# A gated scan and two MLPs in one kernel on one Trainium2 core: subtractions moved to GpSimd, the first pair's rows in 4 KB pieces, f rows and sigmoids earlier, and other ways out for two last blocks

## The chip, the core and the metric

The kernel runs on one core of a Trainium2 chip. TensorE multiplies matrices, VectorE and ScalarE work element by element and read the matmul results from PSUM, GpSimd works element by element from SBUF, and SyncE only issues transfers. Transfers are also issued by ScalarE and GpSimd; each issuer has a queue of its own, and each engine runs its instructions in the order of the program. The metric is the device time of one execution in microseconds (us).

## The reference, cut to what matters

```python
f = lower_bound + (1.0 - lower_bound) * sigmoid(f_logit)   # x, f_logit: 6080 tokens x 256
i = 1.0 - f
for t in range(6080):                                      # the gated scan
    h = f[t] * h + i[t] * x[t]
    y[t] = h
h = y @ w_in                                               # 256 x 2048
y = (h * sigmoid(1.702 * h)) @ w_out                       # layer 1, 2048 x 256
h = y @ w_in_2
g = h if h >= 1 else (0 if h <= -1 else (h + 1) ** 2 / 4)
out = g @ w_out_2                                          # layer 2
```

The weights come as 64-bit floats, 2 words of 32 bits each; x, f_logit and the result are 32-bit.

## The kernel before

**Tiling.** The 6080 tokens are six pairs of two blocks; a block has 480 tokens in the first pair and 512 in the others. Features lie on the 128 partitions, two halves of 128, and tokens along the rows. Every matrix operand is kept as a high half rounded for TensorE (`h`) and a low half, the difference to the exact value (`l`); a product is three matmuls, `wh*mh`, `wl*mh` and `wh*ml` (`three`, L406). ScalarE makes the high half as a cast (L191 for weights, L517 for activations), VectorE the low half as a subtraction (L195 for weights, L521 for activations).

**Order.** The order of all engines is written out by hand. The work of one pair is eight groups of 256 of the 2048 inner columns. The first pair uses `plain_group`: for each of four pieces (P11, P21, P12, P22: block b, half u of the inner columns) two products into a bank, then the down products of the group before, and then whatever `run(s, k)` holds for group s, place k. Later pairs, and all of layer 2, use `group`, which needs seven products for the same result in place of eight. `also(s, k, ...)` and `in_place(4 * s + k, ...)` put work into these places.

**The start.** Before group 0 stands a written order: weight units are loaded and taken from their 64-bit form (`take_apart`, `scale_exponent`, `put_together`, `weight_value`, then `weight_high` and `weight_low`); unit ("i", 0, 0) first, ("i", 0, 1) and ("o", 0, 0) half way. There are 16 units in layer 1, j = 0 to 7 of "i" and "o"; the 15 behind the first are spread over the groups of the first pair, where seven staging tiles take the loads. The blocks of the first pair are loaded by rows (`load_rows`, SP, pieces of 512 bytes), turned by TensorE's transposes (`turn_half`, L286), and scanned: `start_gate` (sigmoid, ScalarE, from PSUM), `forget`, `start_input` (VectorE), `scan` (VectorE), `scan_high`, `scan_low`. The blocks of later pairs are loaded by `load_tokens` in 128-byte pieces, four transfers each, in a blocked order that VectorE's 32 x 32 transposes undo; `sigmoid_tokens` does the sigmoid in place on ScalarE. The sigmoid and the Gelu need different tables of ScalarE, so `sigmoid_tokens` inside the groups has a table load before it, and the next Gelu has another one. The tiles of `load_rows` and `load_tokens` share two buffers each for x and f.

**The ends.** `keep_block` takes the result of a block out of PSUM when its last down product is done. In layer 1 it is copied to two `ev` tiles (halves e = 0 on ScalarE, L469, e = 1 on VectorE, L471) and written to a scratch in DRAM, from which `fetch` reads it for layer 2; the tag `ev` has two buffers. In layer 2 it is turned by VectorE's 32 x 32 transposes (L479) and written in 128-byte pieces, four transfers a block; the last pair's by SP and ScalarE in turn. The last block of all goes half by half through `store_half` (L489, L491), in eight transfers by SP and ScalarE.

Of the kernel before, what the change touches and what calls it, by code (L numbers as in the profile page):

```python
# [14 lines left out]
P = 128  # L15
Q = 32
# [28 lines left out]
def tile_gated_scan_two_mlps(  # L45
# [147 lines left out]
    def weight_low(u):  # L193
        high, low = unit_parts(u)
        nc.vector.tensor_tensor(low, joined.pop(u), high.bitcast(F32), ALU.subtract)  # L195
# [73 lines left out]
    def load_rows(what, b, g):  # L269

        t0, n = blocks[b]
        m = n // 4
        if g == 0:
            raw[what, b] = pool.tile([P, ND, 4, P], F32, tag=f"r{what}", bufs=2, name=f"rows_{what}{b}")
        nc.sync.dma_start(
            out=raw[what, b][:m, g],
            in_={"x": x, "f": f_logit}[what][t0 : t0 + n, g * P : (g + 1) * P].rearrange(
                "(c p) d -> p c d", p=m
            ),
        )  # L280

    def turn_half(b, g, places):
        m = blocks[b][1] // 4
        for what, p in zip("fx", places):
            for c in range(4):
                nc.tensor.transpose(  # L286
                    p[:, c * m : (c + 1) * m], raw[what, b][:m, g, c], ident[:m, :m]
                )
            turned[what, b, g] = p[:, : 4 * m]
# [3 lines left out]

    def start_gate(b, g):
        t = small("e0", "gate", b, g)
        nc.scalar.activation(t, turned.pop(("f", b, g)), AF.Sigmoid, scale=-1.0)
# [9 lines left out]
    def start_input(b, g):  # L306
        if g == 0:
            states[b] = [small("g", "state", b, h, 4) for h in range(ND)]
        nc.vector.scalar_tensor_tensor(
            states[b][g],  # L310
            gates.pop((b, g)),
# [149 lines left out]
    def keep_block(q, b):  # L461
        n = pairs[q % NPAIR][1]
        if q < NPAIR:
            between[q, b] = dram.tile([P, ND, n], F32, name=f"between{q}_{b}")
            for e in range(ND):
                t = pool.tile([P, n], F32, tag="ev", bufs=2, name=f"ev{q}_{b}_{e}")
# [6 lines left out]
        elif q == 2 * NPAIR - 1 and b:  # L473
            for e in range(ND):
                store_half(q, b, e)
        else:
# [3 lines left out]
            for k in range(P // Q):  # L480
                (nc.sync if q < 2 * NPAIR - 1 else (nc.sync, nc.scalar)[k % 2]).dma_start(
# [4 lines left out]
    def store_half(q, b, e):  # L486
        n = pairs[q % NPAIR][1]
        o = pool.tile([P, n], F32, tag=f"e{e}", bufs=2, name=f"o{q}_{b}_{e}")
        nc.vector.transpose(out=o, in_=ys.pop((q, b, e))[:, :n])  # L489
        for k in range(P // Q):  # L490
            (nc.sync, nc.scalar)[k % 2].dma_start(  # L491
                out=blocked(out, 2 * (q - NPAIR) + b, k)[:, e],
                in_=o[k * Q : (k + 1) * Q].rearrange("i (j c) -> i j c", c=Q),
            )
# [24 lines left out]
    def low(s, piece):  # L519
        h, l = parts[s, piece]  # L520
        nc.vector.tensor_tensor(l, G.pop((s, piece)), h.bitcast(F32), ALU.subtract)  # L521
# [149 lines left out]
    for n, (k, u) in enumerate(first_units):  # L671
        begun = {("i", 1): 4, ("o", 0): 3}.get((u[0], u[2]), 0)
# [192 lines left out]
```

## Time and profile before

| | |
|---|---|
| Time, median of 3 runs (lowest to highest) | 1035.28 us (1034.01 to 1037.02) |
| The profiled execution's own time | 1033.54 us |
| Its span, first to last instruction | 1031.7 us |
| TensorE busy | 998.3 us, 97% of the span |
| ScalarE, VectorE, GpSimd busy | 81%, 76%, 4% |
| Mean granted TensorE clock | 0.991 of full |
| Bytes moved | 71.77 MB, of which read from HBM 46.99 MB |

A busy TensorE counts matmuls that overlap, so 97% busy is not 97% of the peak; where it waits and where its clock falls is seen only by stretches. The rows below are of this one profiled execution; its own time is its span and 1.84 us around it.

### The profile page before, as it was taken

What the parts mean: (1) busy time and instruction counts of PE and PEld (TensorE: products, weight loads), DVE (VectorE), ACT (ScalarE), POOL (GpSimd) and SP (SyncE); (2) the same over time, 40 slices, a digit from 0 to 9 for tenths busy, and PEclk for the clock granted to TensorE, in tenths of its full rate; (3) what the DMA queues carried; (4) which work ended last, traced back from release to release, by engine and by line L of the source; (5) the groups of instructions that cost most, each with busy time, mean ns of one, the idle gap of its engine ahead of it and who ended that gap; (6) DMA issues with size and microseconds to landing.
All of it is one profiled execution on the core that took longest, in us unless ns stands there. A gap on an engine that the chain in (4) does not pass through costs nothing.

```text
span 1031.7 us, 12311 instructions
## 1 busy us (share of the span) xinstructions
PE 998.3 (97%) x4378; PEld 823.3 (80%) x4378; DVE 780.0 (76%) x1299; ACT 839.0 (81%) x1439; POOL 45.6 (4%) x80
## 2 busy tenths in 40 slices
PE   6799999999999999999999999999999999999995
PEld 4677888888888888888878888888888888888884
DVE  7889879778868878866667677768768767776664
ACT  5756787887887797877779889989988989998884
POOL 1100000000000000012210000000000000000000
PEclk9899999999999999999999999999999999999998
DMA  9932141054163351244561012002002002002002
GB/s 262 181 62 42 49 69 23 11 129 102 57 155 79 82 123 77 77 160 187 188 210 39 1 46 35 21 21 41 21 21 41 21 22 41 1 1 42 1 1 41
DMA packets 152278, 71.77 MB, mean 70 GB/s; under 512 B 134681, under 2 KB 139033, under 8 KB 152217
## 3 DMA queue, kind: packets, MB, share of 16 engines
q1 hardware_dynamic: 139528, 34.29, 16.6%
q0 software_dynamic: 8496, 36.18, 10.4%
q10 hardware_dynamic: 4192, 0.52, 0.3%
q8 instruction: 34, 0.56, 0.2%
q14 instruction: 28, 0.22, 0.1%
HBM read 46.99 MB, written 23.99 MB: 69 GB/s over the span
## 4 chain that ended last, share of the span: by engine, by line
PE 85%; DVE 6%; ACT 4%; DMA 2%; issue 1%; SPq 1%; DVEq 0%; ACTq 0%; POOLq 0%
PE y L406 45%; PE bank_b L406 17%; PE bank_a L406 11%; PE bank_c L406 11%; ACT gh L517 1%; ACT c L536 1%; ACT c L535 1%; DMA raw_x<-in_x 1%; DVE gl L521 1%; SPq L327 1%; DMA between<-ev 1%; DVE c L543 1%; DMA lb<-in_lower_bound 0%; DVE state L353 0%; DVE fieldsi L168 0%
## 5 line engine op out<-in xcount | busy, mean ns | idle before, releaser
L573 DVE TENSOR_TENSOR h<-bank_c,u 128x512 f32<-128x512 f32 (+1 forms) x176 | 120.4, 684 | 92.9 <-PE bank_c L406 63.9
L521 DVE TENSOR_TENSOR gl<-c,gh 128x512 fp32r<-128x512 f32 (+1 forms) x192 | 130.6, 680 | 10.9 <-ACT gh L517 8.7
L517 ACT CAST gh<-c 128x512 fp32r<-128x512 f32 (+1 forms) x192 | 117.6, 612 | 10.1 <-DVE c L543 9.7
L536 ACT ACTIVATE c<-c 128x512 f32<-128x512 f32 (+1 forms) x192 | 120.6, 628 | 6.1
L521 DVE TENSOR_TENSOR gl<-g,gh 128x512 fp32r<-128x512 f32 (+1 forms) x112 | 75.5, 675 | 42.8 <-ACT gh L517 42.4
L543 DVE SCALAR_TENSOR_TENSOR c<-c,h 128x512 f32<-128x512 f32 (+1 forms) x96 | 65.6, 684 | 55.9 <-ACT c L536 55.9
L531 ACT ACTIVATE h<-h 128x512 f32<-128x512 f32 x80 | 50.5, 631 | 56.7 <-DVE h L573 56.3
L517 ACT CAST gh<-g 128x512 fp32r<-128x512 f32 (+1 forms) x112 | 68.7, 613 | 15.8 <-PE y L406 12.6
L535 ACT ACTIVATE c<-h,half 128x512 f32<-128x512 f32 (+1 forms) x96 | 68.6, 715 | 9.0 <-DVE h L573 9.0
L593 ACT COPY bank_b<-bank_a 128x512 f32<-128x512 f32 (+1 forms) x88 | 50.3, 571 | 24.6 <-PE bank_a L406 23.9
L644 ACT COPY u<-bank_b 128x512 f32<-128x512 f32 (+1 forms) x88 | 50.9, 579 | 17.8 <-PE bank_b L406 17.5
L521 DVE TENSOR_TENSOR gl<-h,gh 128x512 fp32r<-128x512 f32 x80 | 54.8, 684 | 4.7 <-ACT gh L517 4.3
L517 ACT CAST gh<-h 128x512 fp32r<-128x512 f32 x80 | 49.7, 622 | 2.5
L623 ACT COPY u<-bank_b 128x512 f32<-128x512 f32 (+1 forms) x88 | 50.9, 578 | 0.1
L543 DVE SCALAR_TENSOR_TENSOR c<-c,bank_a 128x512 f32<-128x512 f32 (+1 forms) x48 | 32.7, 682 | 18.4 <-ACT c L536 18.4
L406 PE MATMUL y<-gh,wo_1l 128*128 128x512 f32 (+1 forms) x96 | 38.0, 396 | 1.4 <-DVE wo_1l L195 1.4
L406 PE MATMUL y<-gh,wo_0h 128*128 128x512 f32 (+1 forms) x96 | 37.5, 391 | 1.6 <-ACT gh L517 1.6
L406 PE MATMUL y<-gl,wo_5h 128*128 128x512 f32 (+1 forms) x96 | 37.3, 388 | 1.2 <-DVE gl L521 1.2
L406 PE MATMUL y<-gl,wo_2h 128*128 128x512 f32 (+1 forms) x96 | 37.4, 390 | 1.0 <-DVE gl L521 1.0
L406 PE MATMUL y<-gl,wo_3h 128*128 128x512 f32 (+1 forms) x96 | 37.3, 388 | 0.7 <-DVE gl L521 0.7
L406 PE MATMUL y<-gl,wo_0h 128*128 128x512 f32 (+1 forms) x96 | 37.3, 388 | 0.6 <-DVE gl L521 0.6
L406 PE MATMUL y<-gl,wo_1h 128*128 128x512 f32 (+1 forms) x96 | 37.9, 395 | 0.0
(377 smaller groups left out, 2953.8 us busy)
## 6 DMA issues: line engine op xcount, KB each, us to landing
kepti<-ahead_pi POOLq DMA_DIRECT2D x8, 896.0 KB, 3.9
stageo<-in_moe_w_out POOLq DMA_DIRECT2D x13, 512.0 KB, 4.2
stagei<-in_moe_w_in POOLq DMA_DIRECT2D x12, 512.0 KB, 4.2
raw_f<-in_f_logit SPq DMA_DIRECT2D x40, 128.0 KB, 4.2
raw_x<-in_x SPq DMA_DIRECT2D x40, 128.0 KB, 4.0
between<-ev SPq DMA_DIRECT2D x20, 256.0 KB, 2.7
y<-between SPq DMA_DIRECT2D x10, 512.0 KB, 3.4
out_y<-o SPq DMA_DIRECT2D x34, 128.0 KB, 3.5
```

The source lines that it names most:

```text
L327: nc.sync.dma_start(out=t[q * Q : (q + 1) * Q].rearrange("i g (j c) -> i g j c", c=Q), in_=blocked({"x": x, "f": f_logit}[what], b, q),)
L406: nc.tensor.matmul(o, lhsT=w, rhs=m, start=first and i == 0, stop=last and i == 2, skip_group_check=free,)
L517: nc.scalar.copy(parts[s, piece][0], G[s, piece])
L521: nc.vector.tensor_tensor(l, G.pop((s, piece)), h.bitcast(F32), ALU.subtract)
L531: nc.scalar.activation(G[s, piece], h, AF.Gelu_apprx_sigmoid)
L535: nc.scalar.activation(c, h, AF.Relu, scale=0.5, bias=half)
L536: nc.scalar.activation(c, c, AF.Square)
L543: nc.vector.scalar_tensor_tensor(c, c, 1.0, h, ALU.min, ALU.max)
L573: nc.vector.tensor_tensor(h, bank_c[:, : tokens(s)], u, ALU.add)
L593: nc.scalar.copy(b, a)
L623: nc.scalar.copy(u2, b)
L644: nc.scalar.copy(u3, b)
```

## The change

- `weight_low` and, in the first pair, `low` for the piece P21 run on GpSimd and no longer on VectorE (16 and 8 subtractions).
- `load_rows` loads a whole block in one transfer with 4 KB a partition, four tokens after one another. `turn_half` transposes from it, and `in_rows` views put the tokens back in order where ScalarE and VectorE read the transposes out of PSUM.
- f of blocks 2 and 3 is loaded by SP behind the first two weight units and ahead of the next four. `sigmoid_tokens` for them stands in the written order before group 0, ahead of the Gelu table. The steps of unit ("i", 0, 1) all stand before group 0, the last scan stands ahead of them, and the scans of the second pair come one to two places earlier.
- The last block of layer 1 is copied to the tiles `stagei` and `stageo`, which the weight units used before, instead of `ev`.
- In layer 2, two of the four transfers of the last pair's first block go by GpSimd instead of ScalarE. The last block is copied out by ScalarE and VectorE, turned to tokens by eight TensorE transposes, copied out again and written in 1 KB pieces by one transfer of ScalarE and one of SP (`store_last`).

```diff
@@ -192,7 +192,7 @@
 
     def weight_low(u):
         high, low = unit_parts(u)
-        nc.vector.tensor_tensor(low, joined.pop(u), high.bitcast(F32), ALU.subtract)
+        nc.gpsimd.tensor_tensor(low, joined.pop(u), high.bitcast(F32), ALU.subtract)
 
 
     def weight_sums(v):
@@ -266,17 +266,13 @@
     forgets = {}
     states = {}
 
-    def load_rows(what, b, g):
+    def load_rows(what, b):
 
         t0, n = blocks[b]
-        m = n // 4
-        if g == 0:
-            raw[what, b] = pool.tile([P, ND, 4, P], F32, tag=f"r{what}", bufs=2, name=f"rows_{what}{b}")
+        raw[what, b] = t = pool.tile([P, 4, D], F32, tag=f"r{what}", bufs=2, name=f"rows_{what}{b}")
         nc.sync.dma_start(
-            out=raw[what, b][:m, g],
-            in_={"x": x, "f": f_logit}[what][t0 : t0 + n, g * P : (g + 1) * P].rearrange(
-                "(c p) d -> p c d", p=m
-            ),
+            out=t[: n // 4],
+            in_={"x": x, "f": f_logit}[what][t0 : t0 + n, :].rearrange("(p c) d -> p c d", c=4),
         )
 
     def turn_half(b, g, places):
@@ -284,16 +280,19 @@
         for what, p in zip("fx", places):
             for c in range(4):
                 nc.tensor.transpose(
-                    p[:, c * m : (c + 1) * m], raw[what, b][:m, g, c], ident[:m, :m]
+                    p[:, c * m : (c + 1) * m], raw[what, b][:m, c, g * P : (g + 1) * P], ident[:m, :m]
                 )
-            turned[what, b, g] = p[:, : 4 * m]
+            turned[what, b, g] = p[:, : 4 * m].rearrange("q (c p) -> q p c", c=4)
 
     def small(tag, what, b, g, bufs=2):
         return pool.tile([P, blocks[b][1]], F32, tag=tag, bufs=bufs, name=f"{what}{b}_{g}")
 
+    def in_rows(t):
+        return t.rearrange("q (p c) -> q p c", c=4)
+
     def start_gate(b, g):
         t = small("e0", "gate", b, g)
-        nc.scalar.activation(t, turned.pop(("f", b, g)), AF.Sigmoid, scale=-1.0)
+        nc.scalar.activation(in_rows(t), turned.pop(("f", b, g)), AF.Sigmoid, scale=-1.0)
         gates[b, g] = t
 
     def forget(b, g):
@@ -307,8 +306,8 @@
         if g == 0:
             states[b] = [small("g", "state", b, h, 4) for h in range(ND)]
         nc.vector.scalar_tensor_tensor(
-            states[b][g],
-            gates.pop((b, g)),
+            in_rows(states[b][g]),
+            in_rows(gates.pop((b, g))),
             one_minus_lb[:, g : g + 1],
             turned.pop(("x", b, g)),
             ALU.mult,
@@ -463,7 +462,10 @@
         if q < NPAIR:
             between[q, b] = dram.tile([P, ND, n], F32, name=f"between{q}_{b}")
             for e in range(ND):
-                t = pool.tile([P, n], F32, tag="ev", bufs=2, name=f"ev{q}_{b}_{e}")
+                if q == NPAIR - 1 and b:
+                    t = pool.tile([P, n], F32, tag=("stagei", "stageo")[e], name=f"ev{q}_{b}_{e}")
+                else:
+                    t = pool.tile([P, n], F32, tag="ev", bufs=2, name=f"ev{q}_{b}_{e}")
                 y = ys.pop((q, b, e))[:, :n]
                 if e == 0:
                     nc.scalar.copy(t, y)
@@ -471,27 +473,45 @@
                     nc.vector.tensor_copy(t, y)
                 nc.sync.dma_start(out=between[q, b][:, e], in_=t)
         elif q == 2 * NPAIR - 1 and b:
-            for e in range(ND):
-                store_half(q, b, e)
+            store_last(q, b)
         else:
             o = pool.tile([P, ND, n], F32, tag="rf", bufs=2, name=f"o{q}_{b}")
             for e in range(ND):
                 nc.vector.transpose(out=o[:, e], in_=ys.pop((q, b, e))[:, :n])
             for k in range(P // Q):
-                (nc.sync if q < 2 * NPAIR - 1 else (nc.sync, nc.scalar)[k % 2]).dma_start(
+                (nc.sync if q < 2 * NPAIR - 1 else (nc.sync, nc.gpsimd)[k % 2]).dma_start(
                     out=blocked(out, 2 * (q - NPAIR) + b, k),
                     in_=o[k * Q : (k + 1) * Q].rearrange("i g (j c) -> i g j c", c=Q),
                 )
 
-    def store_half(q, b, e):
-        n = pairs[q % NPAIR][1]
-        o = pool.tile([P, n], F32, tag=f"e{e}", bufs=2, name=f"o{q}_{b}_{e}")
-        nc.vector.transpose(out=o, in_=ys.pop((q, b, e))[:, :n])
-        for k in range(P // Q):
-            (nc.sync, nc.scalar)[k % 2].dma_start(
-                out=blocked(out, 2 * (q - NPAIR) + b, k)[:, e],
-                in_=o[k * Q : (k + 1) * Q].rearrange("i (j c) -> i j c", c=Q),
-            )
+    def store_last(q, b):
+
+        t0, n = blocks[2 * (q - NPAIR) + b]
+        m = n // 4
+        rows = out[t0 : t0 + n, :].rearrange("(c p) d -> p c d", p=m)
+        turn = [bank_a, bank_b[LAST % 2 ^ 1]]
+        for e in range(ND):
+            t = pool.tile([P, n], F32, tag=f"e{e}", bufs=2, name=f"last{e}")
+            y = ys.pop((q, b, e))[:, :n]
+            if e == 0:
+                nc.scalar.copy(t, y)
+            else:
+                nc.scalar.copy(t[:, : n // 2], y[:, : n // 2])
+                nc.vector.tensor_copy(t[:, n // 2 :], y[:, n // 2 :])
+            for c in range(4):
+                nc.tensor.transpose(
+                    turn[c // 2][:m, (c % 2) * D + e * P : (c % 2) * D + (e + 1) * P],
+                    t[:, c * m : (c + 1) * m],
+                    ident,
+                )
+        for k, queue in enumerate((nc.scalar, nc.sync)):
+            o = pool.tile([P, 2, D], F32, tag="g", bufs=4, name=f"o_last{k}")
+            y = turn[k].rearrange("p (c d) -> p c d", c=2)
+            if k == 0:
+                nc.scalar.copy(o[:m], y[:m])
+            else:
+                nc.vector.tensor_copy(o[:m], y[:m])
+            queue.dma_start(out=rows[:, 2 * k : 2 * k + 2], in_=o[:m])
 
     def keep(b):
         for key in [key for key in to_keep if key[1] == b]:
@@ -518,7 +538,7 @@
 
     def low(s, piece):
         h, l = parts[s, piece]
-        nc.vector.tensor_tensor(l, G.pop((s, piece)), h.bitcast(F32), ALU.subtract)
+        (nc.gpsimd if s < NG and piece == P21 else nc.vector).tensor_tensor(l, G.pop((s, piece)), h.bitcast(F32), ALU.subtract)
 
     def begin(s, piece, bank=None):
 
@@ -669,7 +689,7 @@
 
     stages = ("stageo", "f0", "f1", "f2", "f3", "f4", "stagei")
     for n, (k, u) in enumerate(first_units):
-        begun = {("i", 1): 4, ("o", 0): 3}.get((u[0], u[2]), 0)
+        begun = {("i", 1): 6, ("o", 0): 3}.get((u[0], u[2]), 0)
         for i, step in enumerate(
             (take_apart, scale_exponent, put_together, weight_value, weight_high, weight_low)
         ):
@@ -701,13 +721,14 @@
                     also(s - 2, 0, load_tokens, "f", b)
                 also(s + (q > 1), 2, load_tokens, "x", b)
             for k in range(2):
-                also(s + (q > 1), 2 + (q == 1), sigmoid_tokens, 2 * q + k)
+                if q > 1:
+                    also(s + 1, 2, sigmoid_tokens, 2 * q + k)
             for k, (b, g) in enumerate((b, g) for b in (2 * q, 2 * q + 1) for g in range(ND)):
-                at = 4 * s + (5 + 5 * k if q == 1 else 8 + 4 * k)
+                at = 4 * s + (4 + 5 * k if q == 1 else 8 + 4 * k)
                 in_place(at, turn_gate, b, g)
                 in_place(at + 1, forget, b, g)
                 in_place(at + 2, turn_input, b, g)
-                in_place(at + 4 - (q > 1), scan, b, g)
+                in_place(at + 3, scan, b, g)
         else:
             for b in range(2):
                 also(s + 1 if q <= NPAIR + 1 else s - 1, 0, fetch, q, b)
@@ -759,11 +780,13 @@
     nc.gpsimd.dma_start(out=lb, in_=lower_bound.rearrange("(c p) -> p c", p=P))
     load_unit(("i", 0, 0), None, nc.sync)
     for b in range(2):
-        for g in range(ND):
-            load_rows("f", b, g)
-            load_rows("x", b, g)
-    for (_, u), tag in zip(first_units, stages[:-1]):
+        for what in "fx":
+            load_rows(what, b)
+    for i, ((_, u), tag) in enumerate(zip(first_units, stages[:-1])):
         load_unit(u, tag, nc.sync)
+        if i == 1:
+            for b in (2, 3):
+                load_tokens("f", b)
     make_identity(nc, ident)
 
     def y_places():
@@ -812,21 +835,23 @@
     scan(1, 0)
     forget(1, 1)
     scan_high(1, 0)
+    sigmoid_tokens(2)
     start_input(1, 1)
     scan_low(1, 0)
+    scan(1, 1)
+    take_apart(i1)
+    scan_high(1, 1)
+    scale_exponent(i1)
+    scan_low(1, 1)
+    put_together(i1)
+    sigmoid_tokens(3)
     nc.scalar.preload_act_table(AF.Gelu_apprx_sigmoid)
-    take_apart(i1)
-    scan(1, 1)
-    scale_exponent(i1)
-    put_together(i1)
     weight_value(i1)
-    scan_high(1, 1)
-    scan_low(1, 1)
     take_apart(o0)
+    weight_high(i1)
+    weight_low(i1)
     scale_exponent(o0)
     put_together(o0)
-    for b in (2, 3):
-        load_tokens("f", b)
     del states[0], states[1]
 
     for s in range(LAST + 2):
```

## Rows read from the trace of the kernel before

**Rows 1.** The chain that ended last, shares of the span by engine

```profile
PE 85%; DVE 6%; ACT 4%; DMA 2%; issue 1%; SPq 1%; DVEq 0%; ACTq 0%; POOLq 0%
```

**Rows 2.** Windows: stretch, its length, busy us per engine, clock, DMA share, GB/s

```profile
25.00:112.00 87.00, 77.16 (x328) 64.26 (x329) 76.82 (x141) 57.28 (x98) 6.51 (x9) 0.94 0.48 92
...
75.00:85.00 10.00, 9.92 (x46) 8.25 (x44) 9.38 (x18) 7.00 (x13) 0.00 (x0) 1.00 0.00 0
...
45.00:55.00 10.00, 9.42 (x31) 8.03 (x32) 7.39 (x14) 4.84 (x10) 0.72 (x1) 0.67 0.48 125
```

**Rows 3.** Waits of TensorE, 0 to 45 us: total us, times, longest

```profile
PE bank_b L406 <- DVE wi_2l L195: 2.4, 1, 2.4
PE bank_b L406 <- DVE wi_1l L195: 2.2, 1, 2.2
```

**Rows 4.** Waits of TensorE, 45 to 125 us

```profile
PE y L406 <- DVE gl L521: 3.3, 4, 1.2
PE y L406 <- DVE wo_1l L195: 1.4, 1, 1.4
```

**Rows 5.** Waits of VectorE, 25 to 112 us

```profile
DVE gl L521 <- ACT gh L517: 9.7, 6, 4.8
```

**Rows 6.** Timeline of the first pair: start, us, engine, line, operation, count, idle before

```profile
13.20 18.03 SPq L327 DMA_DIRECT2D raw_f<-in_f_logit  x8
...
30.39 0.60 PE L406 MATMUL y<-gh,wo_0h 128*128 128x480 f32 x1
...
30.48 1.28 ACT L335 ACT_TABLE_LOAD   x1
...
35.47 1.06 ACT L335 ACTIVATE raw_f<-raw_f 128x1024 f32<-128x1024 f32 x1 [2.64 <-DMA raw_f<-in_f_logit]
...
37.84 0.57 ACT L531 ACTIVATE g<-bank_b 128x480 f32<-128x480 f32 x1
...
113.90 0.39 PE L406 MATMUL bank_a<-x,wi_0h 128*128 128x512 f32 x1
```

**Rows 7.** Windows with three kinds of transfer, columns as in rows 2

```profile
6.00:12.00 6.00, 5.28 (x20) 3.44 (x20) 5.41 (x11) 4.04 (x8) 0.73 (x1) 1.00 1.13 229
...
15.00:20.00 5.00, 4.95 (x17) 3.44 (x15) 4.86 (x8) 3.57 (x5) 0.00 (x0) 1.00 1.05 387
...
43.00:45.00 2.00, 1.18 (x6) 0.69 (x4) 2.00 (x5) 1.07 (x2) 0.72 (x1) 0.95 1.03 163
```

**Rows 8.** Timeline of the first 16 us

```profile
4.99 0.43 DVE L153 TENSOR_SCALAR fieldsi<-stagei 128x512 uint32<-128x512 uint32 x1 [4.09 <-DMA stagei<-in_moe_w_in]
...
14.31 1.06 PE L286 MATMUL bank_b<-ident,rows_x 120*128 120x120 f32 x4
```

**Rows 9.** Groups of VectorE's instructions: count, busy us, mean ns, idle before

```profile
L195 DVE TENSOR_TENSOR wo_0l<-valueo,wo_0h 128x512 fp32r<-128x512 f32 x1 | 0.7, 684 | 0.0
```

**Rows 10.** Timeline of GpSimd, 2 to 26 us

```profile
2.40 0.29 POOL masks.py:199 TENSOR_SCALAR_AFFINE_SELECT ident<-ident 128x128 f32<-128x128 f32 x1
...
21.74 0.72 POOL L135 DMA_DIRECT2D stageo<-in_moe_w_out  x1 [12.87 <-DVE fieldsi L171]
```

**Rows 11.** Timeline of the layer boundary, 534 to 541 us

```profile
538.35 0.59 ACT L469 COPY ev<-y 128x512 f32<-128x512 f32 x1 [3.81 <-DMA between<-ev]
...
538.93 0.69 DVE L471 COPY ev<-y 128x512 f32<-128x512 f32 x1 [4.84 <-DMA between<-ev]
...
539.48 0.48 PE L406 MATMUL y<-gh,wo_0h 128*128 128x480 f32 x1 [1.61 <-ACT gh L517]
...
540.81 0.49 PE L406 MATMUL y<-gl,wo_0h 128*128 128x480 f32 x1 [0.64 <-DVE gl L521]
```

**Rows 12.** Timeline of the end, 1021 us to the end of the span

```profile
1021.26 0.39 PE L406 MATMUL y<-gl,wo_7h 128*128 128x512 f32 x1
...
1022.46 5.68 SPq L491 DMA_DIRECT2D out_y<-o  x4
```

**Rows 13.** Transfers: issuer, count, KB each, median us from issue to landing

```profile
out_y<-o SPq DMA_DIRECT2D x34, 128.0 KB, 3.5
```

## The prediction, made before the changed kernel was run

> **What bounds the kernel now.** I read the page's chain of work that ended last first: 85% of the span runs through TensorE's matmuls [rows 1]. So time can only come from places where TensorE waits, runs at the lower clock, or has finished. I then cut the start into windows. In 75 to 85 us 46 matmuls take 10.0 us, 0.217 us each; that is the full pace of the first pair. From 25 to 112 us VectorE is busy 76.8 of 87.0 us, and in 45 to 55 us the granted clock is 0.67 of 2.4 GHz, a mix of that level and 1.2 [rows 2]. Next the waits of TensorE: 2.4 and 2.2 us for the low halves of weights (wi_2l, wi_1l) [rows 3], then 3.3 us in four waits for low halves of activations and 1.4 us for wo_1l [rows 4]. All of them are VectorE subtractions, L195 and L521. VectorE itself idles there only while it waits for ScalarE's gh, 9.7 us in six waits [rows 5]. The timeline shows why: ScalarE changes its table at 30.48 us, does one sigmoid, waits 2.64 us for the second block's rows, does it, changes the table back, and starts its next Gelu at 37.84 us. Those rows were issued by SP only at 13.20 us, eight transfers in 18.03 us [rows 6].
>
> Size of what can be won at the start: TensorE begins the first down product at 30.39 us and group 8 at 113.90 us [rows 6], 83.5 us. Between them lie 7 groups of 48 matmuls less the 6 of group 1 already done, 330; at 0.217 us that is 71.7 us. So 11.8 us are lost. Two more places: at the layer boundary ScalarE and VectorE wait 3.81 and 4.84 us for a transfer out of `ev`, and TensorE loses 1.61 and 0.64 us behind them [rows 11]. At the end the last matmul starts at 1021.26 us and lasts 0.39 us, yet the span goes to 1031.7 us: 10.0 us of copies and of transfers, four of which take SP 5.68 us to issue from 1022.46 us on [rows 12], with four more on ScalarE's queue beside them.
>
> **The change, part by part.** *Rows of 4 KB.* The first pair's x and f are 4 x 480 KB = 1.97 MB. In 6 to 12 us, when they move in 512-byte pieces, the rate is 229 GB/s; in 15 to 20 us, with 2 KB pieces of weights, 387 GB/s [rows 7]. At the second rate 8.6 us become 5.1: what lies behind in SP's queue comes 3.5 us earlier. Against that, the first x block now lies behind the whole of f, 240 KB more, 0.6 us at 387 GB/s. The transposes read four-token strides and the results are written by views of four; the same instructions stay, 8 reads of PSUM by ScalarE and VectorE. I take no price (bound: 0.6 us on each of the four that lie in the scan chain, 2.4 us).
>
> *Early f rows and sigmoids.* SP now issues the 8 f transfers of blocks 2 and 3 before i2, o1, i3 and o2. They must wait for the buffers of blocks 0 and 1, so for the transposes: four take 1.06 us, there are eight such sets, and the last starts at 14.31 us [rows 8]. SP does nothing else meanwhile, and the weights behind it wait too. The working: i0 is in by 4.99 us [rows 8], the rows by 10.1; i1, o0 and the unit that GpSimd loads, 1.57 MB at 387 GB/s, by 14.2; a block of f, 0.52 MB in 128-byte pieces at the 163 GB/s of 43 to 45 us [rows 7], 3.2 us each, by 17.4 and 20.6; the four weight units, 2.1 MB, 5.4 us more, by 26.0, about when the first of them is taken apart. ScalarE does the sigmoids under the table it already has: two table loads of 1.28 us, the 2.64 us wait and two sigmoids of 1.06 us leave the middle of group 0, 7.3 us between 30.48 and 37.84 [rows 6]. In the new place they stand before `scan_high(1, 1)` and before the first Gelu. So that Gelu is about 1 us later, while the last scan, no longer behind `take_apart`, is 0.6 us earlier. For the point where the first down product starts I take no gain (bounds: 2 us either way).
>
> *GpSimd.* 16 weight subtractions and 8 of P21 leave VectorE; one costs it 0.684 us [rows 9]. 22 lie in 25 to 112 us, at 0.66 us 14.5 us: VectorE falls from 76.8 to 62.3 us, below the 71.7 us that TensorE needs. GpSimd's price is not shown. The nearest row is a one-input select of 128 columns, 0.29 us [rows 10]: four times that, 1.16 us, for 512 columns; with two inputs read one after the other 2.3 us. I take 1.2 to 1.5, because fixed cost does not grow; three a group are under 5 of 10.4 us, and GpSimd has only weight loads otherwise. A load queued behind one comes 1 to 3 us later, with seven stages in hand. Of the 11.8 us I take that the four waits for gl (3.3 us) come back in some form and the rest goes: wi_2l 2.4, wo_1l 1.4, 3.3 for the clock (0.33 x 10 us) and scattered pitch. Gain 8.5 us (bounds 0 and 11.8).
>
> A row cannot say whether the two engines hinder each other, as no GpSimd arithmetic runs beside VectorE here. The Trainium skill speaks against the move: by "SBUF — State Buffer", section "Who interferes with whom", a VectorE instruction with two SBUF inputs and a GpSimd instruction that reads SBUF exclude each other for the whole instruction. By that rule the sum would lose most of its first term (second rival). "GPSIMD Engine Reference", section "Elementwise — side-by-side cycle accounting", gives 4497 ns for 2048 columns, an estimate of 1.1 to 1.2 us for 512; no run here shows it yet.
>
> *Boundary.* The last block of layer 1 gets tiles of its own. The 3.81 and 4.84 us waits have no cause left, the two copies run near 534.5 us, and 1.61 + 0.64 us of TensorE's waits go: 2.3 us (bounds 0, if backlog on ScalarE only moves, and 2.5).
>
> *End.* Block 1 becomes two ScalarE copies, half a VectorE copy, 8 transposes on TensorE, two copies out and two transfers of 256 KB in 1 KB pieces. From the last matmul's end, 1021.65: half a copy 0.35, four transposes 1.06 [rows 8], a copy 0.6, an issue 0.5, landing 3.5 (the median of `out_y` [rows 13]), about 1 to the end of the span: 1028.7. Block 0 keeps its 128-byte pieces, but two of its four transfers go by GpSimd's queue. One of 256 pieces costs GpSimd 0.72 us [rows 10]; one of 1024 pieces lies between that and four times it, 2.9 us. Two end by 1022.5 to 1026.9, landed 3.5 later and with 1 us to the end 1027.0 to 1031.4. I take 1028.4 for both: 3.3 us gained (bounds: 4.7 gained; 4 lost if GpSimd's issues are held like raw_f's longest, about 5 us each).
>
> Sum: the profiled execution has 1033.54 us, 1.84 more than its span; less 8.5, 2.3 and 3.3 it is 1019.4. It lies 1.7 below the runs' median of 1035.28, so against that 1021.2.
>
> **Rivals.** *The tail is not shortened.* GpSimd's small pieces end last. For it: no row has such a transfer. Against it: 0.72 us for 256 pieces. Then 1035.3 - 8.5 - 2.3 + (0 to 4) = 1024.5 to 1028.5.
>
> *GpSimd and VectorE exclude each other.* Then VectorE's stretch is 62.3 + 22 x 1.16 = 87.8 us against 87.0 before, less some 5 us in which it transposes with one input: 0 to 4 us gained at the start instead of 8.5. With the other two terms 1025.5 to 1029.7; I put 1027.7. This is also what the start gives if the sigmoids hold `scan_high(1, 1)` for 5 us more, as they would if the f rows came by 27 us. For it: nearly every VectorE instruction of this stretch has two SBUF inputs. Against it: nothing in the trace; only the fact that VectorE's idle 9.7 us would absorb some.
>
> *Slower.* The same exclusion with a dearer GpSimd instruction. VectorE may grow by 5.6 us before it eats the other two terms: (87.0 + 5.6 - 62.3) / 22 = 1.38 us per instruction is the break-even. At 1.7 us it is 62.3 + 37.4 = 99.7, 12.7 us longer, and 1042 in all; at 1.5 us 1038.
>
> **How the numbers follow.** The forecast 0.52 (its own range 1016 to 1027), the exclusion at 1.16 us 0.28, the tail 0.10, the slower one 0.10. A measurement of this kernel tells 0.3%, 3.1 us, from no change. The first three are all faster but for the outer edge of the second (0.02) and of the third (0.01); the last is 0.03 within 0.3% and 0.07 slower: 0.87, 0.06, 0.07. Leaving out 1 in 10 at the top and about as much at the bottom, the range is 1015.5 to 1031.
>
> **What would show it.** Right: no ScalarE table load between the first Gelu and group 8; L195 on GpSimd at 1.1 to 1.5 us, with L521 still near 0.65 us beside it; wi_2l and wo_1l gone from TensorE's waits; group 8 near 105 us; no wait at the copies of ev near 534 us; less than 8 us after the last matmul. Wrong: VectorE's two-input instructions lengthened or delayed while GpSimd runs, f rows landing after 25 us, the boundary's waits under another name, or GpSimd's transfer as the last to land.

## The result, and the profile after

The changed kernel takes 1041.67 us (median of 7 runs, 1039.06 to 1044.0), the kernel before 1035.28 us beside it (7 runs, 1030.15 to 1038.91): ratio 1.007, 95% interval 1.0043 to 1.0096. It is slower, and the measured time lies 20 us above the forecast of 1021.2 us and outside its range (1015.5 to 1031). The profiled execution of the changed kernel has a span of 1040.76 us against 1031.74. (Two executions below, the profiled one of x10 at 1546 us with a granted clock of 0.608 and one of the kernel before beside x5 to x8 at 2036 us, count in the medians, which they move by less than 0.4 us, but not in the ratios.)

Two marks cut the span at the same work into three stretches: the first product of group 8, and the end of the last down product.

| Stretch | before | after | difference | forecast |
|---|---|---|---|---|
| start of the span to group 8 | 113.90 | 124.84 | +10.94 | -8.5 |
| group 8 to the end of the last down product | 907.75 | 905.13 | -2.62 | -2.3 |
| from there to the end of the span | 10.09 | 10.78 | +0.69 | -3.3 |

The boundary term held, the other two did not. The start divides again: the first down product begins 4.98 us later (35.37 against 30.39 [rows 6]), and from there to group 8 it takes 89.47 us against 83.51. The timeline of the changed kernel in the first pair (start, us, engine, line, operation; in brackets the idle time before and what ended it):

```profile
11.62 11.17 SPq L326 DMA_DIRECT2D raw_f<-in_f_logit  x8
...
22.87 1.06 ACT L334 ACTIVATE raw_f<-raw_f 128x1024 f32<-128x1024 f32 x1 [3.24 <-DMA raw_f<-in_f_logit]
...
26.37 1.06 ACT L334 ACTIVATE raw_f<-raw_f 128x1024 f32<-128x1024 f32 x1 [1.33 <-DMA raw_f<-in_f_logit]
27.45 1.28 ACT L848 ACT_TABLE_LOAD   x1
...
29.89 0.55 ACT L551 ACTIVATE g<-bank_b 128x480 f32<-128x480 f32 x1
...
35.37 0.77 PE L405 MATMUL y<-gh,wo_0h 128*128 128x480 f32 x1 [3.16 <-ACT wo_0h L191]
...
124.84 0.39 PE L405 MATMUL bank_a<-x,wi_0h 128*128 128x512 f32 x1
```

ScalarE waits 3.24 and 1.33 us for the early f rows, and its first Gelu comes at 29.89 us; in the kernel before it came at 23.74. The f rows are late because of what stands ahead of them in SP's queue: the rows of 4 KB moved no faster than the 512-byte pieces did, 230 GB/s where those had 229 [rows 7]. The last of these rows lands at 14.15 us, unit ("o", 0, 0) behind them at 19.77, and the first f transfer right after it at 20.02, though SP had issued it at 11.62. The eight f transfers then land 0.7 to 1.0 us apart, the three issued long before like the five issued just then, so SP's 11.17 us of issuing did not set their time. The windows of the changed kernel (columns as in rows 2), the first from group 1 to group 8:

```profile
30.49:124.84 94.35, 79.64 (x337) 65.76 (x338) 83.65 (x123) 54.02 (x96) 34.98 (x30) 0.93 0.34 68
30.00:117.00 87.00, 71.80 (x301) 59.17 (x302) 76.39 (x109) 48.97 (x87) 34.02 (x29) 0.92 0.37 76
6.00:12.00 6.00, 3.31 (x16) 2.97 (x17) 3.11 (x7) 2.51 (x5) 1.77 (x2) 1.00 1.02 230
```

and that of the kernel before from group 1 to group 8:

```profile
25.48:113.90 88.42, 79.06 (x337) 65.89 (x338) 78.24 (x143) 58.11 (x99) 6.49 (x9) 0.94 0.47 90
```

The stretch from group 1 to group 8 has the larger loss, 5.93 of the 10.94 us. VectorE has 123 instructions in it and is busy 83.65 us; with 20 instructions more, it was busy 78.24 us there in the kernel before. Its instructions have become longer. The changed kernel's timeline shows it one by one:

```profile
32.34 2.32 DVE L179 SCALAR_TENSOR_TENSOR valueo<-fieldso 128x512 f32<-128x512 f32 x1
32.90 1.21 POOL L541 TENSOR_TENSOR gl<-g,gh 128x480 fp32r<-128x480 f32 x1
...
34.70 0.62 ACT L191 CAST wo_0h<-valueo 128x512 fp32r<-128x512 f32 x1 [2.54 <-DVE valueo L179]
...
35.39 1.41 POOL L195 TENSOR_TENSOR wo_0l<-valueo,wo_0h 128x512 fp32r<-128x512 f32 x1 [1.29 <-ACT wo_0h L191]
35.59 1.49 DVE L156 TENSOR_SCALAR fieldso<-stageo 128x512 uint32<-128x512 uint32 x1
```

L179 takes 0.68 us by itself; with a GpSimd subtraction inside it, it is recorded with 2.32 us, ScalarE waits 2.54 us for its result, and TensorE's first down product 3.16 us for ScalarE's (the first timeline). From 30 to 126 us VectorE has 14 records of more than 1.3 us. Each overlaps a subtraction of GpSimd and ends 0.28 to 1.08 us after it, a little less than such an instruction takes by itself (0.42 to 1.27 us), as if it had only begun when GpSimd was done. Three 32 x 32 transposes, which read one input, overlap a subtraction too and keep their 0.70 us. The groups of VectorE (count, busy us, mean ns, idle before) in 30 to 117 us:

```profile
L541 DVE TENSOR_TENSOR gl<-g,gh 128x480 fp32r<-128x480 f32 x20 | 16.7, 834 | 10.3 <-ACT gh L537 10.2
L179 DVE SCALAR_TENSOR_TENSOR valueo<-fieldso 128x512 f32<-128x512 f32 x7 | 8.1, 1163 | 0.0
L179 DVE SCALAR_TENSOR_TENSOR valuei<-fieldsi 128x512 f32<-128x512 f32 x6 | 4.1, 682 | 0.0
...
L338 DVE STREAM_TRANSPOSE gate<-raw_f 128x512 f32<-128x512 f32 x4 | 2.8, 700 | 0.0
```

and of GpSimd, whose 24 subtractions take 33.9 us in sum, 1.21 to 1.76 us each, 1.41 in the mean:

```profile
L541 POOL TENSOR_TENSOR gl<-g,gh 128x480 fp32r<-128x480 f32 x8 | 10.2, 1277 | 38.8 <-ACT gh L537 38.8
L195 POOL TENSOR_TENSOR wo_2l<-valueo,wo_2h 128x512 fp32r<-128x512 f32 x1 | 1.8, 1756 | 0.0
```

TensorE's waits in 50 to 125 us now are (those of before: rows 4)

```profile
PE y L405 <- DVE gl L541: 10.1, 4, 3.5
PE y L405 <- POOL wo_1l L195: 0.4, 1, 0.4
```

so the wait for wo_1l went from 1.4 to 0.4 us (that for wi_2l, before 50 us, from 2.4 to 0.3), as forecast, and the wait for gl, the low half that VectorE mostly still makes, grew from 3.3 to 10.1. The granted clock of the stretch is 0.93, where it was 0.94.

At the layer boundary the copies run without the waits of rows 11 (3.81 and 4.84 us):

```profile
545.61 0.69 DVE L473 COPY ev<-y 128x512 f32<-128x512 f32 x1
...
546.05 0.60 ACT L471 COPY ev<-y 128x512 f32<-128x512 f32 x1
...
546.70 0.38 PE L405 MATMUL y<-gh,wo_0h 128*128 128x480 f32 x1
```

TensorE, which lost 1.61 and 0.64 us behind them, has no wait in 540 to 556 us.

At the end, the timeline and the transfers (issuer, count, KB each, us from issue to landing) of the changed kernel:

```profile
1029.37 1.30 SPq L482 DMA_DIRECT2D out_y<-o  x2
1029.58 0.40 PE L405 MATMUL y<-gl,wo_7h 128*128 128x512 f32 x1
1029.63 1.66 POOL L482 DMA_DIRECT2D out_y<-o  x2 [482.87 <-DVE o L480]
...
1031.53 0.41 ACTq L514 DMA_DIRECT2D out_y<-o_last  x1
1032.09 0.40 SPq L514 DMA_DIRECT2D out_y<-o_last  x1
```

```profile
out_y<-o_last ACTq DMA_DIRECT2D x1, 256.0 KB, 6.0
out_y<-o_last SPq DMA_DIRECT2D x1, 256.0 KB, 6.1
```

All issues are out 2.5 us after the last product (6.6 before), yet the last landing is at 1038.21 us, since the large transfers take 6.0 and 6.1 us where 3.5 was taken [rows 13]. And the span does not end with it: GpSimd's closing drain, the record with which an engine ends its work, runs from 1030.13 to 1039.99 us, 1.3 us after SP's own. In the kernel before, GpSimd's drains are records of 0.1 us.

### The profile page after: what moved, and what is told of

It is laid out like the page before. It is cut to its first block, busy times and chain, and to the rows that moved or that the text cites. A ratio compares the mean times of both kernels' runs of the same rounds, so it can differ in the third digit from the quotient of the medians.

```text
span 1040.8 us, 12331 instructions
## 1 busy us (share of the span) xinstructions
PE 999.1 (96%) x4386; PEld 825.3 (79%) x4386; DVE 784.9 (75%) x1275; ACT 837.6 (80%) x1440; POOL 80.7 (8%) x106
## 4 chain that ended last, share of the span: by engine, by line
PE 86%; DVE 6%; ACT 4%; DMA 1%; issue 1%; POOL 0%; SPq 0%; DVEq 0%; ACTq 0%; POOLq 0%
PE y L405 46%; PE bank_b L405 17%; PE bank_a L405 12%; PE bank_c L405 11%; DVE gl L541 1%; ACT gh L537 1%; ACT c L555 1%; ACT c L556 1%; DMA lb<-in_lower_bound 1%; DVE raw_x L352 1%; DVE c L563 1%; DVE fieldso L168 0%; DMA raw_f<-in_f_logit 0%; DVE valuei L179 0%; DVE fieldso L171 0%
## 5 line engine op out<-in xcount | busy, mean ns | idle before, releaser
L405 PE MATMUL y<-gl,wo_4h 128*128 128x512 f32 (+1 forms) x96 | 37.3, 388 | 1.9 <-DVE gl L541 1.9
L405 PE MATMUL y<-gh,wo_0l 128*128 128x512 f32 (+1 forms) x96 | 37.9, 395 | 0.7 <-POOL wo_0l L195 0.7
```

Source lines behind the costliest of these rows:

```text
L405: nc.tensor.matmul(o, lhsT=w, rhs=m, start=first and i == 0, stop=last and i == 2, skip_group_check=free,)
```

## The experiments

Three sets, each timed beside the kernel before on one chip: x1 to x4 (before 1033.66 us), x5 to x8 (1035.28), x9 to x12 (1035.31).

**The subtractions back on VectorE, all else as changed (x1).**

```diff
-        nc.gpsimd.tensor_tensor(low, joined.pop(u), high.bitcast(F32), ALU.subtract)
+        nc.vector.tensor_tensor(low, joined.pop(u), high.bitcast(F32), ALU.subtract)
...
-        (nc.gpsimd if s < NG and piece == P21 else nc.vector).tensor_tensor(l, G.pop((s, piece)), h.bitcast(F32), ALU.subtract)
+        nc.vector.tensor_tensor(l, G.pop((s, piece)), h.bitcast(F32), ALU.subtract)
```

> The changed kernel with all 24 subtractions back on VectorE, all else as changed. Theory A (GpSimd and VectorE exclude each other, and this is what costs the groups of the first pair): from the start of group 1 to that of group 8 it takes no more than the 88.4 us of the kernel before, against 94.4 in the changed one; no VectorE instruction over 1.3 us; the time falls by 6 to 12 us to 1030 to 1036. Theory B (the new order ahead of group 0 costs it all, GpSimd is harmless): VectorE is fuller, the groups take as long or longer, the time stays within 3 us of 1041.7.

1032.3 us, ratio 0.998 (0.9955 to 1.0004), as theory A said: without the GpSimd arithmetic the changed kernel is level with the one before, and by the two ratios 0.9%, 9.3 us, faster than with it. Group 1 to group 8:

```profile
29.66:115.23 85.57, 78.40 (x337) 64.90 (x337) 78.88 (x144) 53.87 (x96) 6.50 (x9) 0.94 0.42 88
```

VectorE does 21 instructions more than in the changed kernel in 4.8 us less. Taking 21 x 0.66 us out of 78.88 should leave 65.0; it was 83.65. So 18.6 us were put into the others, 0.89 us for each of the 21 GpSimd subtractions of the stretch.

**The subtractions alone on the kernel before (x2): the same two lines, the other way.**

> The kernel before with the 24 subtractions on GpSimd and nothing else. Theory A: VectorE instructions with two SBUF inputs last up to 2.3 us beside GpSimd, group 8 starts 4 to 8 us later than at 113.9, the time is 1039 to 1043. Theory B: VectorE is relieved, the waits for wi_2l, wi_1l and gl go, group 8 starts 5 to 9 us earlier, the time is 1026 to 1031.

1040.6 us, ratio 1.0088 (1.0059 to 1.0118), +9.1 us with an interval of 6.1 to 12.2 (the medians are 6.9 apart), as theory A said: within that width the part by itself costs what it costs inside the change. Group 1 to group 8 takes 93.17 us against 88.42, with VectorE busy 82.22 us in 121 instructions.

**The subtractions added and not moved (x3).** The kernel before keeps all its work on VectorE; GpSimd does the 24 subtractions once more into a tile that nobody reads.

```diff
+    vain = const.tile([P, MAXN], F32, name="vain")
...
+        nc.gpsimd.tensor_tensor(vain, joined[u], high.bitcast(F32), ALU.subtract)
...
+        if s < NG and piece == P21:
+            nc.gpsimd.tensor_tensor(vain[:, : tokens(s)], G[s, piece], h.bitcast(F32), ALU.subtract)
```

> The kernel before, with the same 24 subtractions made once more by GpSimd into a tile that nobody reads; VectorE keeps its own. Nothing waits for GpSimd's results, so only sharing can cost. Theory A: VectorE loses some 15 to 25 us of the 30 us that GpSimd computes, and the time is 1045 to 1060. Theory B: within 3 us of 1035.3. A third case, that GpSimd costs only by the lateness of its results, also gives no change here.

1060.12 us, ratio 1.0269 (1.0236 to 1.0302), +27.8 us, at the upper edge of theory A's range, for work on an engine that is idle otherwise and that nobody waits for by data. VectorE's groups in 20 to 125 us:

```profile
L169 DVE SCALAR_TENSOR_TENSOR fieldsi<-stagei,fieldsi 128x512 uint32<-128x512 uint32 x7 | 11.4, 1622 | 0.0
...
L169 DVE SCALAR_TENSOR_TENSOR fieldso<-stageo,fieldso 128x512 uint32<-128x512 uint32 x7 | 4.8, 682 | 0.5 <-ACT fieldso L164 0.5
```

One line, one shape: 1622 ns in the mean for the units of "i", six of which overlap a subtraction of GpSimd, 682 ns for those of "o", none of which does. In 20 to 140 us no wait of TensorE, VectorE or ScalarE is put down to GpSimd: VectorE's instructions themselves are longer, and ScalarE and TensorE wait for VectorE.

**Copies in place of these subtractions (x9): GpSimd reads one input.**

```diff
-        nc.gpsimd.tensor_tensor(vain, joined[u], high.bitcast(F32), ALU.subtract)
+        nc.gpsimd.tensor_copy(vain, joined[u])
...
-            nc.gpsimd.tensor_tensor(vain[:, : tokens(s)], G[s, piece], h.bitcast(F32), ALU.subtract)
+            nc.gpsimd.tensor_copy(vain[:, : tokens(s)], G[s, piece])
```

> The kernel before, with 24 GpSimd instructions added of the same shapes and at the same places as the added subtractions of the run that gave 1060.12 us, but copies: one input is read, not two, and the target is the same tile that nobody reads. (It computes nothing less.) Theory A, GpSimd keeps VectorE's instructions with two inputs waiting whatever it does itself: 24 copies of some 1 us or more cost VectorE about as much as the subtractions did, in proportion to their length: the time rises by 12 us or more, and VectorE's instructions of 0.68 us beside a copy are recorded with 1.3 us or more. Rival B, only a GpSimd instruction that itself reads two inputs does: the time stays within 3 us of before, and VectorE's durations beside the copies stay at 0.68 us.

1039.08 us, ratio 1.0048 (1.0024 to 1.0071), +5 us: between the two theories. GpSimd's groups and VectorE's:

```profile
L196 POOL COPY vain<-valuei 128x512 f32<-128x512 f32 x8 | 7.7, 960 | 15.2 <-DVE valuei L180 15.1
```

```profile
L197 DVE TENSOR_TENSOR wo_7l<-valueo,wo_7h 128x512 fp32r<-128x512 f32 x1 | 1.1, 1099 | 0.0
...
L197 DVE TENSOR_TENSOR wo_5l<-valueo,wo_5h 128x512 fp32r<-128x512 f32 x1 | 0.7, 679 | 0.0
```

B falls in its strict form: a copy holds VectorE too, L197 takes 1.10 us beside one. But it adds 0.42 us where a subtraction added about 1.0 (L197 had 1.7 in x3), and the sum is 5 us, not 12. A copy is 0.88 us in the mean, a subtraction 1.61 in x3, but GpSimd's records hold waiting as well: most copies run on for 0.4 to 0.6 us after a VectorE instruction that they overlap has ended. The shortest records, 0.59 us for a copy and 1.27 for a subtraction in x3, differ by 0.68, about as much as what they add to VectorE. Why the whole cost falls further, to 0.18 of that of x3, is not settled; the copies need no high half and so start at other moments.

**The two ends alone on the kernel before (x4), and without GpSimd's queue (x5).**

```diff
-                (nc.sync if q < 2 * NPAIR - 1 else (nc.sync, nc.gpsimd)[k % 2]).dma_start(
+                nc.sync.dma_start(
```

> The kernel before with the two ends of the change alone: own tiles for the last block of layer 1, GpSimd's queue for half of the last pair's first block, the transposed last block. Theory A: the boundary gives back 2.3 to 3 us, the end costs about 0.8 us as in the changed kernel (10.8 us from the last down product to the end of the span against 10.0), together 1033 to 1034. Theory C: the tail was only late because of what came before it, and alone it gives the 3 us forecast: 1029 to 1031.

> The kernel before with the boundary's own tiles and the transposed last block, but no transfer on GpSimd: the last pair's first block goes by SP alone, four issues. Theory A (GpSimd's queue costs the end: its pieces of 128 bytes hold the engines, and its drain ends 1.6 us after SP's): the last down product to the end of the span takes 7 to 8 us against 11.2 in x4 and 10.0 before; with the boundary's 2.4 the time is 1028 to 1030. Theory C (the 128-byte pieces themselves set the end, whoever issues them): 9.5 to 10.5 us, 1031.

x4: 1033.28 us, ratio 0.9997 (0.9978 to 1.0016). x5: 1028.04 us, ratio 0.9934 (0.9913 to 0.9955). Both times are those of theory A, though x5's end is longer than its 7 to 8 us. In the traces the stretch behind the last product is 10.88 us in x4 and 8.64 in x5: 2.2 us. The medians are 5.2 us apart, and both runs spread over 8 us, the kernel before beside them over 8 to 12. Where the other 3 us come from is not shown; the start, which all three kernels share, can give as much (their profiled executions reach group 8 at 113.90 us before, 116.74 in x4 and 117.47 in x5, which is the slowest of x5's runs). x11 measures the queue without that spread.

**4 KB rows with the old order (x6), and on 128 partitions (x7).** x6 is x5 with the change's `load_rows`, `turn_half` and `in_rows`. x7 loads 512 tokens in place of the block's 480, so that all 128 partitions take part; the 32 tokens more are read by nobody.

```diff
-            out=t[: n // 4],
-            in_={"x": x, "f": f_logit}[what][t0 : t0 + n, :].rearrange("(p c) d -> p c d", c=4),
+            out=t,
+            in_={"x": x, "f": f_logit}[what][t0 : t0 + 4 * P, :].rearrange("(p c) d -> p c d", c=4),
```

> x5 with rows of 4 KB on 120 partitions, order otherwise as before. If these rows bring no rate (the changed kernel landed 480 KB in 2.2 to 2.4 us, 216 GB/s) and only put x behind all of f: first transposes at 7.4 us and the first product at 17.4 instead of 15.3; then part of it is absorbed by the waits for f rows and weights, 0 to 2 us slower than x5. If the early stages do not bound the start: equal to x5 within 1 us.

> x6 with the rows loaded on all 128 partitions, 32 tokens more than the block has, which nothing reads: 512 KB a transfer. If 120 partitions are why 4 KB pieces took 280 ns where others of 4 KB took 172: the rate in 6 to 12 us rises to 340 to 390 GB/s, a transfer lands 1.4 us after the one ahead, the first product is at 15.5 to 16.0 us, 1 to 2 us faster than x6. If the source tensors or the piece size are the reason: 216 to 250 GB/s, each transfer 7% later, the first product at 17.8.

x6: 1025.29 us, ratio 0.991 (0.9885 to 0.9935). x7: 1024.48 us (1024.25 to 1024.91), ratio 0.9902 (0.988 to 0.9925), the fastest of all and 1% ahead of the kernel before. Both expectations for x6 were missed, as it is no slower than x5; x7 has the rate that was expected, but gains a little less than 1 us and has its first product at 16.73 us. Windows of x6, then of x7 (group 1 to group 8; 6 to 12 us):

```profile
28.86:111.76 82.90, 76.04 (x337) 63.76 (x337) 78.24 (x143) 57.88 (x99) 6.48 (x9) 0.98 0.49 89
6.00:12.00 6.00, 2.28 (x10) 1.94 (x11) 2.19 (x6) 2.24 (x4) 0.73 (x1) 1.00 0.99 236
```

```profile
26.89:109.78 82.89, 76.26 (x337) 63.87 (x337) 78.23 (x143) 57.86 (x99) 6.48 (x9) 0.98 0.43 87
6.00:12.00 6.00, 4.16 (x20) 3.79 (x21) 4.01 (x8) 2.47 (x5) 0.73 (x1) 1.00 0.98 380
```

The same 4 KB pieces move at 236 GB/s into 120 partitions and at 380 GB/s into 128 (in x7 the window has the first 2 KB pieces of weights too). Yet that is worth 0.8 us only. More may lie in x6 already, 2.75 us below x5 by the medians, but the intervals of x5 and x6 overlap and x5 spreads over 8 us. In the traces x6 reaches group 8 at 111.76 us, although its first product comes 3.4 us later than before, because group 1 to group 8 takes 82.90 us against 88.42: TensorE no longer waits for wi_2l (2.4 us [rows 3]), and the clock of the stretch is 0.98 instead of 0.94. What brings this about is not shown. SP issues the next weights from 3.1 us on and not from 8.15, but they land no earlier (unit ("i", 0, 2) at 20.27 us, before at 19.48).

**Early sigmoids with 512-byte rows (x8: x5 and the change's order) and with rows on 128 partitions (x12: x7 and that order).** The main lines of that order:

```diff
+        if i == 1:
+            for b in (2, 3):
+                load_tokens("f", b)
...
+    sigmoid_tokens(2)
...
+    sigmoid_tokens(3)
     nc.scalar.preload_act_table(AF.Gelu_apprx_sigmoid)
```

> x5 with the changed kernel's order (f rows of blocks 2 and 3 ahead of four weight units, their sigmoids ahead of the Gelu table, unit i1 finished and scans earlier), rows of 512 bytes as before, all arithmetic off GpSimd. If the early sigmoids pay but were hidden by the later rows: first product at 15.3, group 8 at 112 to 113.5 (115.2 in x1), 1 to 2 us faster than x5. If the wait for f rows ahead of the last scan's high half and of the first Gelu costs what the freed middle gives: group 8 at 114 to 116, the time equal to x5 within 1.5 us.

> The kernel of 1024.48 us with the changed kernel's order at the start: f tokens loaded after the second unit, sigmoids of both blocks before the table of Gelu, their scans and weight pieces moved. No arithmetic on GpSimd. Theory A, the early sigmoids wait for transfers that stand behind the weights and hold ScalarE and all that is behind it: 2 to 5 us slower, 1026.5 to 1029.5, with the first down product later than in the kernel of 1024.48 us. Rival B, it was the slow row transfers (2.2 to 2.4 us each on 120 partitions) that made the f tokens late; on 128 partitions they come about 4 us sooner, and the order gains the moved sigmoids' time instead: 1022 to 1024 us.

x8: 1030.44 us, ratio 0.9957 (0.9941 to 0.9972), 2.4 above x5, where 1 to 2 us less than x5, or the same within 1.5, was expected; it lies within x5's spread, so x12 has to decide. x12: 1027.89 us (1027.22 to 1028.61), 3.41 above x7, as A said; its mechanism was half wrong. ScalarE of x12:

```profile
19.70 1.06 ACT L334 ACTIVATE raw_f<-raw_f 128x1024 f32<-128x1024 f32 x1 [1.08 <-DMA raw_f<-in_f_logit]
...
23.53 1.06 ACT L334 ACTIVATE raw_f<-raw_f 128x1024 f32<-128x1024 f32 x1 [1.66 <-DMA raw_f<-in_f_logit]
...
27.05 0.55 ACT L551 ACTIVATE g<-bank_b 128x480 f32<-128x480 f32 x1
```

It waits for f even now that the rows ahead are quick, and its first Gelu is 1.9 us behind that of x7 (25.14). But the first down product is 1.3 us ahead (30.35 against 31.63). The loss comes behind it: 83.42 us to group 8, against 78.15. From group 1 to group 8 the windows give

```profile
27.66:113.77 86.11, 78.52 (x336) 64.86 (x337) 78.90 (x144) 54.01 (x96) 6.52 (x9) 0.94 0.42 87
28.50:38.30 9.80, 7.13 (x17) 5.12 (x16) 9.33 (x19) 7.21 (x14) 2.17 (x3) 0.50 1.14 202
```

a clock of 0.94 against 0.98 in x7: 86.11 x 0.06 less 82.89 x 0.02 is 3.5 us, as much as the stretch is longer (3.2). TensorE waited 1.9 us for a Gelu up to 27.66 us; in the second window the clock is at its lower level (0.50, 1.2 GHz), and in it TensorE waits 2.2 us more, for wo_0l. In x7 the clock is at 1.00 from 33.4 us on, here from 38.6. That these waits brought the clock down was not tested.

**The subtractions on the best start (x10), and GpSimd's queue alone on it (x11): x7 with one part each.**

> The kernel of 1024.48 us (rows of 4 KB on 128 partitions, the two copy-out changes without GpSimd's queue, the order before) with the 24 subtractions moved to GpSimd as in the changed kernel. Theory A, the subtractions cost what they keep VectorE waiting, in any start: 1024.48 + 8 to 10 = 1032 to 1035 us, as they did on the kernel before (+9.1 us by the ratio) and in the changed kernel (9.4 us less without them). Rival B, they cost only where late weight transfers have put VectorE behind: this start has its weights early, and the time stays within 2 us of 1024.5.

> The kernel of 1024.48 us with two of the four transfers of the last pair's first block given to GpSimd's queue, as in the changed kernel; no arithmetic on GpSimd. Theory A, the queue costs at the end alone: the stretch from the last down product to the end of the span grows from 8.2 to about 10.8 us, so 1026.7 to 1027.2 us, and GpSimd's drain ends last. Rival B, GpSimd's queue costs nothing and the 5 us between the two runs of the copy-out changes (1033.28 with it, 1028.04 without) were chance in the start: within 0.7 us of 1024.5. If it is more than 4 us, the queue costs somewhere else too.

x10: 1035.58 us, ratio 0.9999 (0.9978 to 1.0021), 11.10 above x7, a little more than theory A's 8 to 10: early weights don't help. x11: 1027.07 us (1026.74 to 1027.61), ratio 0.9933 (0.9906 to 0.9959), 2.59 above x7, as theory A said. The timeline of x7's end and of x11's:

```profile
1013.73 2.99 SPq L482 DMA_DIRECT2D out_y<-o  x4
1013.93 0.39 PE L405 MATMUL y<-gl,wo_7h 128*128 128x512 f32 x1
1015.87 0.41 ACTq L514 DMA_DIRECT2D out_y<-o_last  x1
1016.81 1.56 SPq L514 DMA_DIRECT2D out_y<-o_last  x1
```

```profile
1013.95 1.30 SPq L482 DMA_DIRECT2D out_y<-o  x2
1014.16 0.40 PE L405 MATMUL y<-gl,wo_7h 128*128 128x512 f32 x1
1014.22 1.66 POOL L482 DMA_DIRECT2D out_y<-o  x2 [482.90 <-DVE o L480]
1016.11 0.41 ACTq L514 DMA_DIRECT2D out_y<-o_last  x1
1016.68 0.40 SPq L514 DMA_DIRECT2D out_y<-o_last  x1
```

SP alone issues the four transfers as fast as it is needed. In x7 the last landing is at 1021.48 us, 7.16 us behind the last product, and the span ends 1.1 us later. In x11 it is at 1022.86, 8.3 behind, and GpSimd's drain, recorded from 1014.72 to 1024.64 us, ends last. So the queue costs twice: the last transfers land later (6.1 and 6.2 us after their issue instead of 3.6 and 4.7), and the drain ends 1.3 us after SP's.

## Why the prediction was wrong

The parts add up, taken as if they did not act on each other. From x7: the subtractions 11.10 (x10), the early order 3.41 (x12), GpSimd's queue 2.59 (x11), 120 partitions instead of 128 0.81 (x6): 1024.48 + 17.91 = 1042.4 us, against 1041.67 measured.

**The step that failed: GpSimd's work was taken to cost VectorE nothing.** The price of one subtraction, "1.2 to 1.5", was right (1.41 in the mean). Wrong was that VectorE "falls from 76.8 to 62.3 us": with its two-input instructions held, it stayed at 76.4 of 87 us (30 to 117 us, the second window). Of the 8.5 us of gain, the waits for wi_2l and wo_1l did shrink (3.8 to 0.7 us), but the 3.3 us for the clock did not come (0.93, before 0.94), and gl, which was to cost its 3.3 us again, cost 10.1. The third rival had this mechanism and a break-even of 1.38 us, and the chip landed on it: by its formula, VectorE's 62.3 + 22 x 1.41 = 93.3 is 6.3 us more than before. The subtractions measured 9.1 (x2, 6.1 to 12.2), 9.3 (x1) and 11.1 us (x10). The formula was too high for VectorE, into which each subtraction put 0.89 us and not its length, and by x1 and x10 too low for the time: what is held is late for TensorE, gl 10.1 us, and wi_1l 3.5 us in x2. That this rival's 1042 us, worked out for 1.7 us an instruction, is nearly the measured time is luck: at 1.41 it gives 1035.3 + 6.3 - 5.6 = 1036, and the rest came from the early order and the end. The slower rival should have had more weight than the exclusion at 1.16 us: the 1.16 was the lower end, worked out from a one-input select, for an instruction with two inputs, and the prediction's own 1.2 to 1.5 lay on both sides of the break-even.

The trace agrees with the Trainium skill, "SBUF — State Buffer", section "Who interferes with whom": a VectorE instruction with two SBUF inputs and a GpSimd instruction that reads SBUF exclude each other (0.68 us became 1.7 to 2.4 us here), one with a single input need not (transposes 0.70 us throughout). By the same section `tensor_scalar` can be among the excluded, and L156 with one input went from 0.42 to 1.49 us. The estimate of 1.1 to 1.2 us from "GPSIMD Engine Reference", section "Elementwise — side-by-side cycle accounting", lies just under the shortest record, 1.21.

**Early rows and sigmoids: "no gain", bounds 2 us either way.** The working had f landing at 17.4 and 20.6 us; it landed at 22.7 and 26.3 (20.0 for the first transfer). The rate at its root failed: 4 KB rows were put at the 387 GB/s of another transfer, and had 230. That is over half of it: in x12, at 380 GB/s, f landed at 19.5 and 23.4, still 2 to 3 us after the working. In x1 the first down product is 1.96 us late, within the bound; in the changed kernel 4.98, and as the two differ by the subtractions alone, the rest is theirs (2.32 us on L179 among it). What the working did not see is the price behind that point: 3.41 us in x12 although the two table loads are gone from the groups, and at a lower clock.

**Boundary: right**, 2.62 us against 2.3, and 3.2 to 3.3 in x5, x6 and x7.

**End: -3.3, measured +0.69.** The work of `store_last` went as forecast, with the last issue at 2.1 us behind the last product. Mis-sized was the landing: 3.5 us taken, 6.1 measured beside GpSimd's pieces, 3.6 and 4.7 without them. GpSimd's issues were cheap, 0.84 us each, in the lower half of the bound; its drain was no term at all. The first rival, the tail not shortened, had the size right (0 to 4 us lost), but by another mechanism: GpSimd's own pieces were not the last to land, at 1036.83 us against 1038.21.

## What to carry to other kernels

An idle GpSimd is no free place for VectorE's work: against a VectorE that runs two-input instructions count most of its length (here 0.89 of 1.41 us) as VectorE's own, and test it by adding the work in vain. A part that is idle at one end (a queue, a drain) still counts if the program ends with it. Put bulk rows on all 128 partitions (0.8 us here), and time the start as a whole: a step that brings the first down product forward can lose more behind it (x12: 1.3 us forward, 5.3 lost, with a lower clock).

## What the runs showed of the hardware that was not expected

- A GpSimd queue with 128-byte pieces at the end: its drain ran 9.9 us (1014.72 to 1024.64) in x11, ending 1.8 us after the last landing, and transfers of ScalarE and SP took 6.1 and 6.2 us to land instead of 3.6 and 4.7.
- 4 KB pieces into 120 partitions moved at 230 and 236 GB/s, into 128 at 380 GB/s.
- GpSimd copies hold VectorE as well, for 0.42 us where subtractions hold it for 1.0; and a one-input instruction of VectorE can be held too (L156, 0.42 to 1.49 us), while transposes were not.
- The spread of the runs changes with the start: 25 runs of the kernel before lie in 1029.71 to 1040.13 us, 11 of x5 in 1024.56 to 1032.36, while x6 and x7 stay within 1.4 and 0.7 us, and x8, with the old rows in the new order, within 2.2. What makes that spread was not tried.
